# The split of the key, value and gate weights into high and low parts, made by GpSimd in place of VectorE

## The chip, the core and the metric

The kernel runs on one core of one Trainium2 chip. The metric is the time of one execution on the device in microseconds (us). Five engines work side by side on the core, each through its own list of instructions in order: TensorE (PE in the profile; its weight loads stand apart as PEld), VectorE (DVE), ScalarE (ACT), GpSimd (POOL) and SyncE (SP, which here only issues transfers). They wait for each other through semaphores.

## The reference

A gated mix of an attention with 32 heads that share one key and one value head, and a gated feed-forward network, over 2048 tokens of width 512:

```python
def _A_ref(x, wq, wk, wv, wo):                     # S = 2048, D = 512, H = 32, Dh = 16
    q = (x @ wq).reshape(B, S, H, Dh).transpose(0, 2, 1, 3)
    k = x @ wk
    v = x @ wv
    scores = jnp.einsum("bhqd,bkd->bhqk", q, k) * (Dh ** -0.5)
    p = softmax(scores, axis=-1)
    o = jnp.einsum("bhqk,bkd->bhqd", p, v)
    return o.transpose(0, 2, 1, 3).reshape(B, S, H * Dh) @ wo

def _B_ref(x, w_gate, w_up, w_down):               # F = 1792
    return (silu(x @ w_gate) * (x @ w_up)) @ w_down

g = sigmoid((x * gate_w).sum(-1, keepdims=True))
return g * _A_ref(x, ...) + (1 - g) * _B_ref(x, ...)
```

All inputs and the output are float32. The factors of the change are `wk` and `wv` (512 x 16 each) and `gate_w` (512).

## The kernel before

Each float32 factor of a product is split into a high part, rounded to the type float32r, and a low part, the difference between the factor and its high part. A product is then the sum of three matmuls: high by high, high by low, low by high. The helper `split(hi, lo, src, eng, eng_hi)` makes the parts with two instructions: a copy on `eng_hi` (L110, a CAST in the profile) and a subtraction on `eng` (L111, a TENSOR_TENSOR). Its defaults are VectorE for the copy and GpSimd for the subtraction.

The change lies in the kernel's opening, which is written out by hand from L675 on under a manual schedule: on each engine the instructions stand in the order of the code. The 2048 tokens are four chunks of 512. In this order:

- `zeros(WARM)` (L614) is 30 matmuls on zeros that fill TensorE's time until the first tokens have come.
- `load_wq(0)` loads the first 128 columns of the query weights into `wraw` and splits them on GpSimd into `wq0h` and `wq0l`, both steps.
- `transpose_x(c, i)` handles half a chunk, tiles `i` and `i + 1`: eight transposes on TensorE (L627) from `xt` into a PSUM tile `pss`, of which there are two; then ScalarE copies the tile to `xh` (L631) and VectorE subtracts to get `xl` (L632), which frees the PSUM tile. In chunk 0 six matmuls on zeros follow each four transposes.
- `prepare_kv()` stands between the two halves of chunk 0. It fills `wkv_h` and `wkv_l`, both 128 x 4 x 113, from `wkv_f`, which holds `wk`, `wv` and `gate_w` as they were loaded. There are four splits: the keys three times over as 128 x 4 x 48 into columns 0 to 47 and again into 64 to 111, the values (128 x 4 x 16) and the gate (128 x 4). That is four copies and four subtractions, all eight on VectorE.
- `project_kv(c)` multiplies a chunk by `wkv_h` and `wkv_l` (12 matmuls at L120): ScalarE copies the result to `vz` (L647), and GpSimd writes the keys' high and low parts into `ks` (L653, L655). `project_kv(0)` comes after both halves of chunk 1 have been transposed, and before chunk 2's transposes.

Then come the queries of the first eight heads (`query(0, c)`, L198, with `wq0h` and `wq0l`), and from about 50 us on the main part: scores (L760), exponentials (L771), the sums over the values (L787) and between them the feed-forward network's matmuls (L198).

A matmul that reads `wkv_h` waits until all four copies have been made, since its 113 columns hold what each of them writes; one that reads `wkv_l` waits for all four subtractions.

Of the kernel before, what the change touches and what calls it, by code (L numbers as in the profile page):

```python
# [65 lines left out]
def tile_gated_mix(ctx, tc, x, wq, wk, wv, wo, w_gate, w_up, w_down, gate_w, out):  # L66
    nc = tc.nc
# [41 lines left out]
    def split(hi, lo, src, eng=nc.gpsimd, eng_hi=nc.vector):  # L109
        eng_hi.tensor_copy(hi, src)  # L110
        eng.tensor_tensor(lo, src, hi.bitcast(F32), ALU.subtract)  # L111
# [459 lines left out]
    with tc.tile_pool(name="apool", bufs=1) as ap, tc.tile_pool(name="apool2", bufs=2) as a2:  # L571
# [9 lines left out]
        wkv_f = ap.tile([P, KD, 2 * DH + 1], F32, name="wkv_f")  # L581
# [6 lines left out]
        wkv_h = ap.tile([P, KD, KW], F32R, name="wkv_h")  # L588
        wkv_l = ap.tile([P, KD, KW], F32R, name="wkv_l")

        def prepare_kv():
            k, v, g = slice(0, DH), slice(DH, 2 * DH), slice(2 * DH, 2 * DH + 1)
            for r in (0, RT):
                to = [w[:, :, r:r + 3 * DH].rearrange("p k (i n) -> p k i n", i=3) for w in (wkv_h, wkv_l)]
                src = wkv_f[:, :, k].unsqueeze(2).to_broadcast([P, KD, 3, DH])
                split(to[0], to[1], src, nc.vector)
            for to, src in ((3 * DH, v), (KW - 1, g)):
                rows = slice(to, to + src.stop - src.start)
                split(wkv_h[:, :, rows], wkv_l[:, :, rows], wkv_f[:, :, src], nc.vector)

        spread = ap.tile([DH, DH, HG], F32, name="spread")

# [72 lines left out]
        with tc.manual_schedule():  # L675
# [5 lines left out]
            load_wq(0)  # L681
            transpose_x(0, 0)
            prepare_kv()
            transpose_x(0, 2)
            prepare_norms()
# [364 lines left out]
```

## Time and profile before

| | |
|---|---|
| median of 3 runs | 1328.92 us (1328.61 to 1329.1) |
| the profiled execution's own time | 1328.69 us |
| its span, first to last instruction | 1326.9 us |
| TensorE, matmuls | busy 1315.6 us, 99% of the span |
| VectorE | 805.4 us, 61% |
| ScalarE | 1077.5 us, 81% |
| GpSimd | 222.9 us, 17%, 229 instructions |

Times in rows of the trace count from the span's start. The timeline's rows give the start, the duration, the engine, the line, the operation and the tiles, and in brackets how long the engine was idle just before and what ended that. A matmul's end is modelled, and matmuls overlap, so that of a row of them the distance between starts tells the pace. The chain is the work that ended last, followed back from the last instruction; its rows in order of time give a start, a length, and the engine and line that filled it.

### The profile page before, as it was taken

The numbers are of one execution on the slowest core, as the hardware profiler recorded it, in microseconds if no ns is written. First come the engines' busy times: TensorE is split into PE (matmuls) and PEld (weight loads), VectorE is DVE, ScalarE is ACT, GpSimd is POOL, SyncE is SP. The second block draws the span as 40 slices with busy tenths as digits, with TensorE's granted clock in tenths as the row PEclk, the third lists the DMA queues.
The fourth block names the chain that finished last, engine by engine and source line by source line (L and its number), as shares of the span: only waits on it lengthen the run. The fifth ranks groups of instructions, "written<-read, shape, count | busy, mean of one in ns | idle before, by whom it ended". The sixth has DMA issues, their size and how long they took to land.

```text
span 1326.9 us, 26852 instructions
## 1 busy us (share of the span) xinstructions
PE 1315.6 (99%) x10767; PEld 786.2 (59%) x10767; DVE 805.4 (61%) x1370; ACT 1077.5 (81%) x1625; POOL 222.9 (17%) x229
## 2 busy tenths in 40 slices
PE   9999999999999999999999999999999999999998
PEld 7655565565555655555655555655555555655677
DVE  4655566566656666666656566566557566666642
ACT  4578888888888888888989889889889888889601
POOL 5350231142031151132110000000000000001043
PEclk9999999999999999999999999999999999999999
DMA  8677021221134373354134252143033252252264
GB/s 287 201 244 232 22 66 37 61 73 56 51 99 149 105 251 108 100 164 139 52 130 164 81 177 87 53 130 102 25 121 104 68 179 69 68 163 77 69 230 148
DMA packets 102513, 157.34 MB, mean 119 GB/s; under 512 B 11888, under 2 KB 43376, under 8 KB 100720
## 3 DMA queue, kind: packets, MB, share of 16 engines
q1 hardware_dynamic: 100656, 155.36, 36.0%
q8 instruction: 88, 1.44, 0.4%
q10 hardware_dynamic: 1728, 0.20, 0.1%
q14 instruction: 41, 0.34, 0.1%
HBM read 99.42 MB, written 55.57 MB: 117 GB/s over the span
## 4 chain that ended last, share of the span: by engine, by line
PE 97%; DVE 2%; ACT 1%; issue 0%; ACTq 0%; DVEq 0%
PE pf L198 38%; PE po L787 34%; PE pss L760 20%; PE pf L120 4%; ACT pt L771 1%; DVE pt L766 1%; PE pss L627 0%; PE po L614 0%; DVE acc L398 0%; DVE hh L110 0%; DVE xl L632 0%; DVE hl L111 0%; PE pss L667 0%; DVE ht L323 0%; DVE ht L333 0%
## 5 line engine op out<-in xcount | busy, mean ns | idle before, releaser
L771 ACT ACTIVATE pt<-pss 128x512 f32<-128x512 f32 (+1 forms) x1024 | 770.2, 814 | 159.9 <-PE pss L760 135.2
L766 DVE COPY pt<-pss 128x512 f32<-128x512 f32 x504 | 348.5, 692 | 366.9 <-PE pss L760 359.8
L787 PE MATMUL po<-pt,vaug 128*32 128x512 f32 x4096 | 461.4, 595 | 0.0
L760 PE MATMUL pss<-qs,ks 64*128 64x512 f32 x2048 | 411.4, 409 | 1.2 <-DVE sign L484 0.7
L760 PEld LDWEIGHTS pss<-qs,ks 64*128 64x128 f32 x2048 | 199.8, 184 | 184.0 <-ACT pt L771 116.5
L787 PEld LDWEIGHTS po<-pt,vaug 128*32 128x32 f32 x4096 | 124.7, 109 | 267.7 <-issue 266.2
L771 ACT ACTIVATE pt<-pt 128x512 f32<-128x512 f32 x504 | 282.0, 629 | 0.0
L198 PE MATMUL pf<-xh,wgh 64*128 64x512 f32 (+1 forms) x444 | 163.9, 393 | 0.5 <-DVE sign L484 0.3
L198 PE MATMUL pf<-xh,wgl 64*128 64x512 f32 (+1 forms) x444 | 164.2, 393 | 0.0
L198 PE MATMUL pf<-xl,wgh 64*128 64x512 f32 (+1 forms) x444 | 163.3, 391 | 0.0
L198 PE MATMUL pf<-xh,wuh 64*128 64x512 f32 (+1 forms) x440 | 160.3, 393 | 0.7 <-DVE sign L484 0.5
L198 PE MATMUL pf<-xh,wul 64*128 64x512 f32 (+1 forms) x440 | 160.2, 392 | 0.0
L198 PE MATMUL pf<-xl,wuh 64*128 64x512 f32 (+1 forms) x440 | 158.3, 391 | 0.0
L198 PE MATMUL pf<-wdh,hh 64*128 64x512 f32 (+1 forms) x411 | 136.4, 393 | 0.1
L198 PE MATMUL pf<-wdh,hl 64*128 64x512 f32 (+1 forms) x411 | 135.7, 391 | 0.0
L198 PE MATMUL pf<-wdl,hh 64*128 64x512 f32 (+1 forms) x411 | 135.4, 390 | 0.0
L798 DVE RECIPROCAL rsb<-rsb 128x128 f32<-128x128 f32 x128 | 116.6, 933 | 1.7 <-issue 0.7
L515 POOL CAST xh<-wraw 128x512 fp32r<-128x512 f32 x4 | 2.9, 732 | 497.0 <-PE pss L760 493.4
L198 PEld LDWEIGHTS pf<-xh,wgh 64*128 64x128 f32 (+1 forms) x444 | 78.9, 185 | 8.3 <-issue 1.1
L198 PEld LDWEIGHTS pf<-xh,wuh 64*128 64x128 f32 (+1 forms) x440 | 77.3, 185 | 10.8 <-DVE sign L484 1.4
L198 PEld LDWEIGHTS pf<-xh,wgl 64*128 64x128 f32 (+1 forms) x444 | 79.1, 185 | 5.5
L198 PEld LDWEIGHTS pf<-xl,wgh 64*128 64x128 f32 (+1 forms) x444 | 79.2, 185 | 5.4
(170 smaller groups left out, 1377.2 us busy)
## 6 DMA issues: line engine op xcount, KB each, us to landing
qs<-q_d SPq DMA_DIRECT2D x31, 512.0 KB, 4.6
q_d<-hh SPq DMA_DIRECT2D x28, 256.0 KB, 3.8
wraw<-in_B_w_gate_dram SPq DMA_DIRECT2D x28, 256.0 KB, 3.7
wraw<-in_B_w_up_dram SPq DMA_DIRECT2D x28, 256.0 KB, 3.2
wraw<-in_B_w_down_dram SPq DMA_DIRECT2D x28, 256.0 KB, 3.3
wgh<-w_d SPq DMA_DIRECT2D x28, 256.0 KB, 2.7
wgl<-w_d SPq DMA_DIRECT2D x28, 256.0 KB, 2.9
wuh<-w_d SPq DMA_DIRECT2D x28, 256.0 KB, 2.7
```

The source lines that it names most:

```text
L120: nc.tensor.matmul(ps, a, b, start=(i == 0), stop=(i == n - 1))
L198: ins = nc.tensor.matmul(self.ps, a, b, start=(i == 0 and opens), stop=(last and closes))
L515: nc.gpsimd.tensor_copy(OT[c][0][:, k, :], raw)
L760: nc.tensor.matmul(ps[:, b * CH:(b + 1) * CH], ks[rows, kt * P:(kt + 1) * P], QS[h][rows, j, :], start=True, stop=True)
L766: other = nc.vector.tensor_copy(pt[:, CH:], ps[:, CH:])
L771: ins = nc.scalar.activation(pt[:, w], ps[:, w], AF.Exp, scale=SCALE)
L787: ins = nc.tensor.matmul(po[c * 2 * DH:(c + 1) * 2 * DH, :], vaug[:, kt, :], pt[:, c * CH:(c + 1) * CH], start=(kt == 0), stop=(kt == NT - 1))
L798: nc.vector.reciprocal(rsb[:, w], rsb[:, w])
```

## The change

In `prepare_kv()` the two calls of `split` name GpSimd for both steps:

```diff
             for r in (0, RT):
                 to = [w[:, :, r:r + 3 * DH].rearrange("p k (i n) -> p k i n", i=3) for w in (wkv_h, wkv_l)]
                 src = wkv_f[:, :, k].unsqueeze(2).to_broadcast([P, KD, 3, DH])
-                split(to[0], to[1], src, nc.vector)
+                split(to[0], to[1], src, nc.gpsimd, nc.gpsimd)
             for to, src in ((3 * DH, v), (KW - 1, g)):
                 rows = slice(to, to + src.stop - src.start)
-                split(wkv_h[:, :, rows], wkv_l[:, :, rows], wkv_f[:, :, src], nc.vector)
+                split(wkv_h[:, :, rows], wkv_l[:, :, rows], wkv_f[:, :, src], nc.gpsimd, nc.gpsimd)
```

On VectorE the eight instructions are gone from between the first and the second `xl` of chunk 0. On GpSimd they come at the place that this piece of its list shows, in the opening (`wraw` is where loaded weights land, DMAHW names a wait for a transfer, Pool, DVE and Activation a wait for an instruction of GpSimd, VectorE or ScalarE):

```order
 L110 CAST wq0h<-wraw 128x512 [waits DMAHW1_49]
 L111 TENSOR_TENSOR wq0l<-wraw,wq0h 128x512 [waits Pool_49]
+L110 CAST wkv_h<-wkv_f 128x4x48 [waits DMAHW0_49]
+L111 TENSOR_TENSOR wkv_l<-wkv_f,wkv_h 128x4x48 [waits Pool_49]
+L110 CAST wkv_h<-wkv_f 128x4x48
+L111 TENSOR_TENSOR wkv_l<-wkv_f,wkv_h 128x4x48 [waits Pool_49]
+L110 CAST wkv_h<-wkv_f 128x4x16 [waits DMAHW2_49]
+L111 TENSOR_TENSOR wkv_l<-wkv_f,wkv_h 128x4x16 [waits Pool_49]
+L110 CAST wkv_h<-wkv_f 128x4 [waits DMAHW4_49]
+L111 TENSOR_TENSOR wkv_l<-wkv_f,wkv_h 128x4 [waits Pool_49]
 L653 CAST ks<-vz 48x512 [waits Activation_49]
 L655 TENSOR_TENSOR ks<-vz,ks 16x512 [waits Pool_49]
```

They stand behind the split of the first query weights, which waits for a transfer, and ahead of the first keys. TensorE's list keeps its order; its waits change where `project_kv(0)` begins:

```order
 L627 MATMUL pss<-ident,xt 128x128 [waits DMAHW0_49,DVE_49]
 L627 MATMUL pss<-ident,xt 128x128 x7
-L120 MATMUL pf<-xh,wkv_h 113x512 [waits Activation_49]
-L120 MATMUL pf<-xh,wkv_l 113x512
+L120 MATMUL pf<-xh,wkv_h 113x512 [waits Activation_49,Pool_49]
+L120 MATMUL pf<-xh,wkv_l 113x512 [waits Pool_49]
 L120 MATMUL pf<-xh,wkv_h 113x512
 L120 MATMUL pf<-xh,wkv_l 113x512
```

The first two matmuls on the key, value and gate weights now wait for GpSimd, where before the first one's wait for VectorE was already covered by the transposes ahead of it.

## The prediction

> **What bounds the kernel now.** I read the page first (busy shares, the chain by engine), then the waits of TensorE, then the chain in order of time through the opening, and last each engine's rows there.
>
> ```profile
> span 1326.9 us, 26852 instructions
> PE 1315.6 (99%) x10767; PEld 786.2 (59%) x10767; DVE 805.4 (61%) x1370; ACT 1077.5 (81%) x1625; POOL 222.9 (17%) x229
> PE 97%; DVE 2%; ACT 1%; issue 0%; ACTq 0%; DVEq 0%
> ```
>
> TensorE is the kernel: 97% of the chain. VectorE's 2% and ScalarE's 1% are places where TensorE stood still. Its waits over the whole span, all that the trace names:
>
> ```profile
> PE pss L627 <- DVE xl L632: 2.2, 2, 1.8
> PE po L614 <- DVE warm L678: 1.0, 1, 1.0
> PE pf L198 <- DVE sign L484: 0.8, 3, 0.3
> PE pss L760 <- DVE sign L484: 0.7, 3, 0.3
> PE pf L198 <- DVE hl L111: 0.4, 1, 0.4
> PE pss L760 <- ACT pt L771: 0.4, 2, 0.2
> PE pf L198 <- DVE hh L110: 0.3, 1, 0.3
> ```
>
> Only the first two lie in the opening (L627 are the transposes, L614 the matmuls on zeros). The other five sum to 2.6 us, and every releaser in them is an engine fed by TensorE itself. None is a transfer. So TensorE's list runs through almost without a break, and an idle microsecond put into it early is not given back later: all else in the kernel is released by TensorE's progress and moves along with it.
>
> The chain through the opening:
>
> ```profile
> 6.66 1.03 ACT xh L631
> 7.70 0.02 issue
> 7.72 1.23 DVE xl L632
> 8.95 0.18 DVE wkv_h L110
> ...
> 10.55 0.17 DVE wkv_l L111
> 10.72 1.14 DVE xl L632
> 11.86 0.04 issue
> 11.91 1.09 PE pss L627 x8
> 13.00 2.78 PE pf L120 x12
> 15.78 1.75 PE pss L627 x16
> ```
>
> The reader is to see two things. The eight instructions of the split are on the chain now: from 8.95 to 10.72 us, 1.77 us, they hold back the second `xl`, and that holds back the transposes of chunk 1's second half. And from 11.91 us on it is TensorE alone: transposes, `project_kv(0)` (12 matmuls), chunk 2's transposes.
>
> **What is taken away.**
>
> ```profile
> 8.34 1.02 ACT L631 ACTIVATE xh<-pss 128x1024 fp32r<-128x1024 f32 x1 [0.65 <-PE pss L627]
> 8.86 0.25 DVE L110 CAST wkv_h<-wkv_f 128x192 fp32r<-128x192 f32 x1
> 9.15 0.36 DVE L111 TENSOR_TENSOR wkv_l<-wkv_f,wkv_h 128x192 fp32r<-128x192 f32 x1
> 10.63 1.22 DVE L632 TENSOR_TENSOR xl<-pss,xh 128x1024 fp32r<-128x1024 f32 x1
> 11.91 1.09 PE L627 MATMUL pss<-ident,xt 128*128 128x128 f32 x8 [1.81 <-DVE xl L632]
> 13.07 0.39 PE L120 MATMUL pf<-xh,wkv_l 128*113 128x512 f32 x1
> ```
>
> Without the eight, the second `xl` waits only for its `xh`, which ends at 8.34 + 1.02 = 9.36. With the 0.03 us that the chain shows between the same two steps (6.66 + 1.03 to 7.72) it starts at 9.39 instead of 10.63, 1.24 us earlier, and ends at 10.61. The transposes of chunk 1's second half start some 0.06 us later (10.63 + 1.22 to 11.91), at 10.67, and are through at 11.76, if their tokens are there by then; the row names `xl` and no transfer as the last that they waited for, and a later landing would change nothing of the sum below. So TensorE could begin `project_kv(0)` 1.2 us earlier than now. What VectorE does next (`sel`, `spread`, `vaug`) only moves forward.
>
> **What is added.** GpSimd takes the eight after `wq0l`:
>
> ```profile
> 11.08 1.06 POOL L110 CAST wq0h<-wraw 128x512 fp32r<-128x512 f32 x1 [8.06 <-DMA wraw<-in_A_wq_dram]
> 12.22 1.56 POOL L111 TENSOR_TENSOR wq0l<-wraw,wq0h 128x512 fp32r<-128x512 f32 x1
> 16.48 0.61 POOL L653 CAST ks<-vz 48x512 fp32r<-48x512 f32 x1 [2.70 <-ACT vz L647]
> 17.16 1.28 POOL L655 TENSOR_TENSOR ks<-vz,ks 16x512 fp32r<-16x512 f32 x1
> ```
>
> The query weights land at 11.08, and nothing in the change touches that transfer. GpSimd is free at 12.22 + 1.56 = 13.78. That is the main point: even eight instructions of no length would be done 0.7 us after `project_kv(0)`'s second matmul starts today (13.07).
>
> Their length is not in the trace; no small copy or subtraction of GpSimd stands in it. The nearest rows:
>
> ```profile
> L111 POOL TENSOR_TENSOR wgl<-wraw,wgh 128x512 fp32r<-128x512 f32 x28 | 36.5, 1305 | 2.2
> L110 POOL CAST wuh<-wraw 128x512 fp32r<-128x512 f32 x28 | 17.2, 613 | 193.5 <-PE pf L198 141.2 <-DMA wraw<-in_B_w_up_dram 40.0 <-PE pss L760 12.3
> L608 POOL MEMSET ks<- 128x2048 f32 x1 | 1.8, 1811 | 0.0
> masks.py:197 POOL MEMSET ident<- 128x128 f32 x1 | 0.2, 206 | 0.3 <-POOLq L1036 0.3
> L1036 POOL MEMSET const-float32-0.0<- 128x1 f32 x1 | 0.1, 99 | 0.2 <-issue 0.2
> ```
>
> The memsets give a base of 0.1 us and (1811 - 206) / 1920 = 0.84 ns per element. A copy of 512 at 0.613 us is then 0.19 + 0.84 ns per element, and a subtraction with the same base 0.19 + (1305 - 190) / 512 = 2.18 ns per element. So 192 elements cost 0.35 and 0.61, 64 cost 0.24 and 0.33, 4 cost 0.19 and 0.20. The four splits sum to 2 x 0.96 + 0.57 + 0.39 = 2.88 us. The pattern in these eight is broken into runs of 16. `wq0h`, whose read jumps at every element, took 1.06 where a plain copy took 0.61; a little of that, and the 0.08 us from a copy's end to its subtraction (11.08 + 1.06 to 12.22), bring me to 3.0 us. The ends: cost in strict proportion to the elements, (192 + 192 + 64 + 4) / 512 x (0.61 + 1.30) = 1.7 us; or each of the eight as dear as a whole 512, 4 x 1.92 = 7.7 us. I stay by the sum because the small memsets are far below a 512's price.
>
> [...]
>
> **The sum.** The last subtraction ends at 13.78 + 3.0 = 16.8. The second matmul of `project_kv(0)`, the first on `wkv_l`, starts about 0.15 us later, at 16.95, in place of 13.07: +3.9 us. The first, on `wkv_h`, waits for the last copy, a step before, and decides nothing. After it TensorE's list runs as before: chunk 2's transposes, `vz`, the keys on GpSimd (idle there for 2.70 us before 16.48, and their release moves by the same 3.9), the query weights behind them. SyncE's list keeps its order; its loads of chunk 3 wait for chunk 1's transposes and go out earlier by 1.2 us, which nobody waits for. The 1.2 us won on VectorE is lost in TensorE's longer wait. Against the profiled execution, 1328.69 + 3.9 = 1332.6; its own time lies 0.23 below the median, so I forecast 1332.8 for the median, +0.29%.
>
> **The rivals.**
>
> *TensorE's clock falls in the new gap.* TensorE would stand still from 11.76 to about 16.6, 4.8 us. The longest gap in the trace so far is 1.81 us, and the pace behind it is full. At the start the pace was half:
>
> ```profile
> 1.00 3.38 PE L614 MATMUL po<-warm 128*128 128x128 bf16 x30 [1.00 <-DVE warm L678]
> 4.17 1.06 PE L627 MATMUL pss<-ident,xt 128*128 128x128 f32 x4
> 6.46 0.50 PE L614 MATMUL po<-warm 128*128 128x128 bf16 x6
> 6.80 0.61 PE L627 MATMUL pss<-ident,xt 128*128 128x128 f32 x4
> ```
>
> Four transposes took 1.06 us and later 0.61; the change falls near 6.4, 5.4 us after TensorE's first matmul. If the gap brings the slow pace back for as long, 5.4 us of work do half of it: 2.7 us more, 1335.5. For it: nothing in the trace shows a gap this long without it. Against: nothing shows that a gap does it. [...] I give this rival 0.32.
>
> *GpSimd's small instructions are cheap* (the other side: not slower by what can be told). The delay is the eight's length plus 0.9 us (13.78 + 0.15 - 13.07). At the strict proportion, 1.7 us, it is 2.6: 1331.5, +0.19%. It decides below 1.8 us for all eight, less than half the price that GpSimd's rows give when VectorE itself needed 1.77. Chance 0.11.
>
> *GpSimd does them in its idle 8 us.* The splits' data are loaded early, GpSimd idles until 11.08, and were they made then, `project_kv(0)` would start 1.2 us earlier: 1327.7. The engine's list decides: they stand behind `wq0h`, and the row shows that instruction waiting for its transfer. Chance 0.02.
>
> *They are dearer* than 4 us together, broken patterns costing a base per run: at the end of 7.7 us the delay is 8.6, 1337.5. `wq0h`'s 0.45 us extra for 64 broken rows speaks for less than 0.1 in 12 rows. Chance 0.05.
>
> **How the numbers follow.** The forecast itself has 0.49. What a measurement can tell from no change is about 0.2%, 2.7 us. Slower by more: 0.49 + 0.32 + 0.05 = 0.86; within: 0.11 + 0.02 = 0.13, since the idle time's 1.2 us are less than the bound; faster: 0.01, for what I have not thought of. The range goes from 1331.5, the proportional price, to 1336.0, the fallen clock's 1335.5 with half a microsecond for GpSimd's price; it leaves out the dear end and what lies below.
>
> **What the changed profile would show.** GpSimd's first `wkv_h` at about 13.7 and the last `wkv_l` ending at 16.8 (their sum 3.0); the second `xl` at 9.39; chunk 1's last transposes at 10.67; TensorE's new wait, about 4.8 us at L120 released by GpSimd's `wkv_l` or `wkv_h`; the second matmul at 16.95; from there every row later by 3.9, with no wait gone at the end. If the clock has fallen, the 12 matmuls behind the gap stand over 0.4 us apart in place of 0.23. The prediction is wrong if the query weights land at another time, if the eight take under 1.8 or over 4 us, or if a later stage takes up the shift.

## The result, and the profile after

| | before | after |
|---|---|---|
| median | 1328.63 us (1328.08 to 1329.1, 6 runs) | 1335.45 us (1334.37 to 1336.06, 6 runs) |
| ratio to before | | 1.0052, 95% interval 1.0042 to 1.0062 |
| the profiled execution's own time and span | 1328.69, 1326.9 us | 1334.83, 1332.8 us |
| mean granted clock of TensorE | 1.000 | 0.997 |

The change made the kernel 6.8 us slower. The forecast was 1332.8; the measured time is that of its first rival, the fallen clock, at 1335.5.

The page of the changed kernel, in the lines that answer to those of before:

```profile
span 1332.8 us, 26854 instructions
PE 1317.8 (99%) x10767; PEld 787.7 (59%) x10767; DVE 804.6 (60%) x1362; ACT 1077.1 (81%) x1625; POOL 225.0 (17%) x237
PEclk8999999999999999999999999999999999999999
```

The busy shares tell next to nothing: VectorE 0.8 us less, GpSimd 2.1 us more. The row of the clock, in tenths per fortieth of the span, does: its first digit is an 8. In the page of before it is a 9:

```profile
PEclk9999999999999999999999999999999999999999
```

The records of the clock begin with its rise (at 4.51 us here, at 6.39 in before), so the slow start of either execution is not in these rows or in the mean. TensorE's longest wait in the changed kernel is new:

```profile
PE pf L120 <- POOL wkv_h L110: 5.0, 1, 5.0
```

The chain in order of time shows what stands ahead of that wait and behind it:

```profile
4.70 6.03 DMA wraw<-in_A_wq_dram
...
10.79 1.06 POOL wq0h L110
...
11.93 1.51 POOL wq0l L111
13.44 0.30 POOL wkv_h L110
...
15.95 0.14 POOL wkv_h L110
16.09 0.04 issue
16.14 5.46 PE pf L120 x12
21.60 1.80 PE pss L627 x16
23.40 2.77 PE pf L120 x12
```

In the place of ScalarE, VectorE and TensorE the chain now has the transfer of the query weights, their split on GpSimd, and the eight instructions behind it. The 12 matmuls of `project_kv(0)` begin at 16.14 us and take 5.46 us; before they began at 13.00 and took 2.78, and the next 12 here take 2.77 again. The sum closes on the two profiled executions: 3.14 us later, 2.68 slower, 0.05 in the transposes, 5.87 of the spans' 5.9 us. The rest of the kernel adds nothing in sum: matmul for matmul the shift is 5.86 us at 33 us, up to 6.4 in between, and 5.84 at the last one.

Next comes the clock. The trace records the moments at which it changes: in the changed kernel at 4.51, 14.75, 21.58 and 1332.30 us. They lie 3, 2 and 384 times 3.413 us apart, and the two in before's trace, at 6.39 and 1327.35 us, 387 times. So the stretches below are steps of that grid (columns: stretch and length, busy time and count of TensorE's matmuls, of its weight loads, of VectorE, ScalarE and GpSimd, the granted clock, the transfers' share and GB/s):

```profile
11.34:14.75 3.41, 0.00 (x0) 0.00 (x0) 1.85 (x2) 0.82 (x1) 3.19 (x5) 1.00 0.96 332
14.75:18.17 3.42, 2.03 (x5) 1.63 (x6) 0.00 (x0) 0.00 (x0) 1.44 (x5) 0.50 0.32 117
18.17:21.58 3.41, 3.41 (x10) 2.37 (x9) 0.00 (x0) 0.00 (x0) 0.00 (x0) 0.50 0.00 0
21.58:25.00 3.42, 3.42 (x25) 3.02 (x24) 2.04 (x3) 2.87 (x4) 2.51 (x3) 1.00 0.00 0
```

TensorE did nothing from 11.34 to 14.75 us; then its clock stood at half for two such steps, and came back after one that was busy throughout. All six runs have a mean clock of 0.996 or 0.997; two steps at half speed in 1333 us make 0.997.

### The profile page after: what moved, and what is told of

The parts are those of the page before. It is cut to its first block, busy times and chain, and to the rows that moved or that the text cites. A ratio compares the mean times of both kernels' runs of the same rounds, so it can differ in the third digit from the quotient of the medians.

```text
span 1332.8 us, 26854 instructions
## 1 busy us (share of the span) xinstructions
PE 1317.8 (99%) x10767; PEld 787.7 (59%) x10767; DVE 804.6 (60%) x1362; ACT 1077.1 (81%) x1625; POOL 225.0 (17%) x237
## 4 chain that ended last, share of the span: by engine, by line
PE 96%; DVE 1%; ACT 1%; DMA 1%; POOL 0%; issue 0%; SPq 0%; ACTq 0%; DVEq 0%
PE pf L198 38%; PE po L787 34%; PE pss L760 20%; PE pf L120 4%; ACT pt L771 1%; DVE pt L766 1%; DMA wraw<-in_A_wq_dram 0%; PE pss L627 0%; DMA wkv_f<-in_A_wk_dram 0%; DVE acc L398 0%; DVE hh L110 0%; PE pss L667 0%; POOL wkv_l L111 0%; POOL wq0l L111 0%; DVE ht L323 0%
```

## The experiments

The theory from here on: the time is lost in two terms, 4.0 us because the split stands behind the query weights' transfer on GpSimd, and 2.7 us because TensorE's clock falls in the gap. The rival: the clock is a by-product, and GpSimd's pace or what follows it costs all of it.

### Zeros in the gap: fill60, fill20, fill40

```diff
             transpose_x(1, 2)
+            zeros(60)
```

> 60 matmuls on zeros are put into TensorE's wait of 5.0 us (11.10 to 16.14 us in the changed kernel's trace), ahead of the first matmul on the key, value and gate weights. At about 0.068 us each (six started 0.41 us before the next transpose) they take some 4.1 us, so that 0.9 us of the wait stay idle and GpSimd's end still decides. Theory (the gap halves TensorE's clock, and the 12 matmuls behind it take 5.46 us in place of 2.78): the 2.7 us come back, 1332.7 us, the 12 matmuls 0.23 us apart, mean clock 1.000. Rival (the slow matmuls are not due to the idle gap, or the time is lost elsewhere): 1335.4 us as before.

Measured: 1332.41 us (1331.15 to 1333.72, 7 runs), ratio 1.0029 (1.0018 to 1.0041) to the kernel before, whose median beside it was 1328.41: +4.0 us, where the change alone has +6.8; the two intervals, 2.4 to 5.4 us and 5.6 to 8.2, do not meet. TensorE's rows in its profile:

```profile
11.32 3.51 PE L614 MATMUL po<-warm 128*128 128x128 bf16 x60
16.36 0.48 PE L120 MATMUL pf<-xh,wkv_h 128*113 128x512 f32 x1 [1.53 <-POOL wkv_h L110]
...
16.97 0.39 PE L120 MATMUL pf<-xh,wkv_h 128*113 128x512 f32 x1
17.20 0.39 PE L120 MATMUL pf<-xh,wkv_l 128*113 128x512 f32 x1
```

The matmuls behind the gap start as late as in the changed kernel, and 0.23 us apart in place of 0.43; the granted clock is 1.00 in the two steps from 11.48 to 18.31 us. The two terms come apart: matmuls that compute nothing of use gave back 2.8 us, the 2.7 of the clock, and left 4.0 us. The rival falls.

> The same with 20 matmuls on zeros, some 1.4 us: a gap of about 3.7 us is left. If the clock falls only when a whole free-running window of 3.41 us (the distance that the records of the clock show) lies in the gap, it falls in about 1 execution of 10, and most runs stand at 1332.7 us with a mean clock of 1.000. If a mostly idle window is enough, as the fall in all six runs with a gap of 5.0 us suggests, it falls in part or all of the runs: those stand near 1335.4 us with a mean clock of 0.997. Rival of no link to the gap: 1335.4 us in all.

Measured: 1334.01 us (1333.35 to 1335.96, 5 runs), ratio 1.0042 (1.0028 to 1.0056). The profiled execution is the slowest of the five, at 1335.96 us. A gap of 3.67 us was left in it, and the clock fell for two steps, behind one that was busy for 20%:

```profile
12.43:15.84 3.41, 0.69 (x13) 0.52 (x10) 1.51 (x2) 0.64 (x1) 3.17 (x6) 1.00 0.96 312
```

So a mostly idle step was enough here, and it was not idle as a whole. The other four runs lie at 1333.35 to 1334.45 us, between the two cases. Whether the clock fell in each of them is not shown, since runs of fill60 reach 1333.72 us with a mean clock of 0.999 or 1.000.

> 40 matmuls on zeros in TensorE's wait, some 2.4 us by the 20 that took 1.28 us and the 60 that took 3.51: a gap of about 2.6 us is left. The profiles so far: the clock fell after a window of 3.41 us in which TensorE was busy for 38% or less (the windows' grid laid on its rows), and not after one with 45% or more. Theory (the fall goes by the share of a window): a gap of 2.6 us leaves a window at 24% at the lowest and 62% at the highest, by where the grid lies, so that the clock falls in part of the runs: these stand near 1335 us, the others at 1332.4 us, with the median between. Rival (a gap below a whole window never lets it fall): 1332.4 us in all.

Measured: 1333.58 us (1332.61 to 1334.24, 5 runs), ratio 1.0036 (1.0022 to 1.005). The gap left was 2.43 us, shorter than one step of 3.41, and in the profiled execution the clock fell all the same, for one step:

```profile
12.88:16.30 3.42, 1.17 (x21) 1.00 (x18) 1.22 (x1) 0.00 (x1) 3.18 (x8) 1.00 0.99 322
16.30:19.71 3.41, 3.23 (x8) 2.47 (x9) 0.00 (x0) 0.00 (x0) 0.34 (x2) 0.50 0.11 42
```

So the gap was not as long as a step either. Whether the clock held in others of its runs can't be read from their times, which lie between the two cases.

### Half of the change: sub_only

```diff
-                split(to[0], to[1], src, nc.gpsimd, nc.gpsimd)
+                split(to[0], to[1], src)
...
-                split(wkv_h[:, :, rows], wkv_l[:, :, rows], wkv_f[:, :, src], nc.gpsimd, nc.gpsimd)
+                split(wkv_h[:, :, rows], wkv_l[:, :, rows], wkv_f[:, :, src])
```

The copies are VectorE's again, and only the subtractions are GpSimd's.

> Half of the change: the four copies stay on VectorE, the four subtractions go to GpSimd. GpSimd is free of the query weights at about 13.4 to 13.8 us, and the four subtractions take 0.60 + 0.59 + 0.32 + 0.21 = 1.7 us: the second matmul on the new weights starts at about 15.3 us in place of 13.07. Theory: +2.2 us for the start, and a gap of about 3 us whose effect on the clock is open: 1330.8 us with the clock held, up to 1333.5 us with a fall. Rival (place in line does not matter, only the amount moved to GpSimd): half of the change's 6.8 us, 1332.0 us, at a full clock.

Measured: 1333.74 us (1332.23 to 1334.68, 4 runs), ratio 1.0039 (1.0024 to 1.0054). By the medians, half of the work costs about three quarters of the loss. The second matmul starts at 15.44 us behind a wait of 3.3 us, close to the 15.3 expected, and the clock fell with the dearer end of my figure. The step ahead of the fall is the busiest one in an opening that led to one, 1.33 us of 3.42, 39%:

```profile
10.37:13.79 3.42, 1.33 (x9) 1.00 (x9) 2.94 (x6) 1.91 (x2) 2.55 (x3) 1.00 0.91 298
13.79:17.20 3.41, 1.76 (x4) 1.37 (x5) 0.45 (x1) 0.00 (x0) 1.60 (x5) 0.50 0.79 299
```

Against it stand two steps of the kernel before on the same kind of grid, busy for 47% and 45%, behind which the clock held:

```profile
9.81:13.22 3.41, 1.60 (x13) 1.30 (x12) 3.34 (x10) 1.21 (x2) 2.05 (x2) 1.00 0.82 280
1320.53:1323.94 3.41, 1.54 (x13) 1.33 (x12) 0.97 (x2) 0.00 (x0) 0.00 (x0) 1.00 0.47 160
```

The end of a kernel, where no work is left to be slowed, narrows the bound. In kv_first, the next experiment, the clock fell at 1321.92 us, behind this step of 44%:

```profile
1318.51:1321.92 3.41, 1.50 (x13) 1.29 (x11) 0.97 (x2) 0.00 (x0) 0.00 (x0) 1.00 0.47 161
```

Of the steps at full clock that are measured here, the clock fell behind those busy for 0, 20, 34, 39 and 44%, and held behind those of 45% and 47% and behind one of 48% in another execution of before (before_look2, 7.31 to 10.72 us).

### GpSimd first the split, then the query weights: kv_first

```diff
-            load_wq(0)
             transpose_x(0, 0)
             prepare_kv()
+            load_wq(0)
```

> GpSimd makes the key, value and gate parts ahead of the first query weights (the load of the query weights is written behind the split; SyncE's list is the same). The last of their three loads lands at some 7.7 us, GpSimd then ends about 8.6 us, before chunk 1's transposes are through. Theory (the loss is GpSimd's place in line behind the wait for the query weights, not GpSimd's pace): no wait of TensorE on GpSimd, no fall of the clock, and the 1.2 to 1.9 us that VectorE's eight instructions held up are won: the first of the 12 matmuls at 11.1 to 11.8 us in place of 13.0, time 1326.7 to 1327.4 us. [...]

Measured: 1328.19 us (1326.57 to 1329.0, 11 runs), ratio 0.9998 (0.9989 to 1.0007). All of the loss is gone, with the same eight instructions on the same engine at the same length:

```profile
4.30 0.35 POOL L110 CAST wkv_h<-wkv_f 128x192 fp32r<-128x192 f32 x1 [1.28 <-DMA wkv_f<-in_A_wk_dram]
...
8.86 0.21 POOL L111 TENSOR_TENSOR wkv_l<-wkv_f,wkv_h 128x4 fp32r<-128x4 f32 x1
11.45 1.10 POOL L110 CAST wq0h<-wraw 128x512 fp32r<-128x512 f32 x1 [2.38 <-DMA wraw<-in_A_wq_dram]
```

They are done at 9.07 us, before TensorE wants them. The loss was the place in GpSimd's line. But the gain that I expected, 1.2 to 1.9 us, did not show.

> The same kernel as kv_first, which had a median of 1328.19 us over 11 runs and a profiled execution of 1326.82 us. Open is whether the 1.2 us that VectorE no longer holds up reach the end. Theory (they do, and the runs so far scatter by as much): 1327.2 us as a median of fresh runs. Rival (the transfers of the tokens set the transposes of chunk 1 in most executions, so that there was little to win): 1328.2 us, and the profile shows the transposes released by transfers.

Measured: 1328.39 us (1327.04 to 1329.99, 11 runs), ratio 0.9998 (0.9989 to 1.0007). The same again, nearer the rival's 1328.2 than the theory's 1327.2, and the profile has what the rival named (steps of issue, 0.02 to 0.04 us each, are left out):

```profile
2.13 5.60 DMA xt<-in_A_x_dram
7.77 0.67 PE pss L627 x4
8.46 1.03 ACT xh L631
9.52 1.24 DVE xl L632
10.80 1.09 PE pss L627 x8
11.89 2.78 PE pf L120 x12
```

Now the transfer of chunk 0's last tokens, landing at 7.73, begins the chain, and the 12 matmuls follow at 11.89 (11.97 in kv_first). That is 1.1 us ahead of the 13.00 of before's profile, which raises the question whether 13.00 is usual.

### Two more executions of the kernel before

> The kernel before itself, for a second profile of its opening. Open is why kv_first, whose 12 matmuls start at 11.7 us in both its profiles, is not 1.3 us faster than before, whose start at 13.0 us is known from one execution. If before's start comes earlier in other executions (where TensorE's clock rises early, the first transposes and with them VectorE's first subtraction come earlier, and the eight instructions behind it fit into the wait for the tokens), this one shows a start at 11.9 to 12.5 us. If 13.0 us is usual, the gain is lost behind the start.

> A third profile of the kernel before, with the same expectation as the second: a start of the 12 matmuls between 11.9 and 12.5 us where the clock rises before 5 us, and near 13.0 us where it rises after 6 us.

Measured: 1328.49 and 1327.36 us, one run each. Their chains, where the 12 matmuls begin:

```profile
11.05 1.09 PE pss L627 x8
12.14 2.78 PE pf L120 x12
```

```profile
10.84 1.09 PE pss L627 x8
11.94 2.77 PE pf L120 x12
```

The start is 12.14 and 11.94, as expected for an early rise of the clock: it rose at 4.6 and 3.9 us in them, against 6.4 in the execution on which the prediction was built, so that the first transposes and VectorE's first subtraction came earlier. What the eight hold up, by the end of the second `xh` and the start of the second `xl` behind it, is 0.1 us in the one, where the tokens came late (`xh` until 9.62, `xl` from 9.77), and 0.9 us in the other, where they came early (8.61 and 9.57), against 1.2 in the first. So there is less to win than one profile said, and kv_first, both of whose profiles have late tokens, wins 0.2 to 0.3 us in the medians, with an interval of 1.2 us to either side. How much of the rest reaches the end stays open.

### VectorE, but later in its line: dve_later

The kernel before with two lines exchanged:

```diff
-            prepare_kv()
             transpose_x(0, 2)
+            prepare_kv()
```

> The kernel before, with the split on VectorE but behind the second half of chunk 0, so that it no longer holds up that half's subtraction. The second subtraction then starts at about 9.4 us and the eight instructions run from about 10.6 to 12.4 us. The first matmul on wkv_h waits for the last copy, at some 12.2 us, in place of 13.0: theory (the place in VectorE's line was the cost, not the engine): 1327.6 to 1328.0 us. Rival (transfers set the pace): 1328.4 us, no difference.

Measured: 1332.07 us (1329.62 to 1333.28, 8 runs), ratio 1.0024 (1.0013 to 1.0034): slower by 3.4 us, against both expectations. VectorE's rows, and GpSimd's of the same stretch:

```profile
11.37 0.36 DVE L111 TENSOR_TENSOR wkv_l<-wkv_f,wkv_h 128x192 fp32r<-128x192 f32 x1
...
11.93 1.09 DVE L111 TENSOR_TENSOR wkv_l<-wkv_f,wkv_h 128x192 fp32r<-128x192 f32 x1
12.95 1.51 DVE L110 CAST wkv_h<-wkv_f 128x64 fp32r<-128x64 f32 x1
...
11.68 1.12 POOL L110 CAST wq0h<-wraw 128x512 fp32r<-128x512 f32 x1 [8.66 <-DMA wraw<-in_A_wq_dram]
12.89 1.51 POOL L111 TENSOR_TENSOR wq0l<-wraw,wq0h 128x512 fp32r<-128x512 f32 x1
```

The second subtraction of 192 took 1.09 us where the first took 0.36, and the copy of 64 took 1.51 where it took 0.19 before. Each started while an instruction of GpSimd ran, and ended just after it: 13.02 against 12.80, 14.46 against 14.40. The query weights' transfer had landed before both. The late start need not be all of the 3.4 us: five of the eight runs have a mean clock of 0.997 or 0.998, the profiled one 0.999, so the clock may have fallen in others, which no trace shows.

> In dve_later VectorE's subtraction of 192 took 1.09 us in place of 0.36 and its copy of 64 took 1.51 in place of 0.19; they ended 0.2 and 0.1 us after GpSimd's copy and subtraction on the first query weights, beside which they had started. Here the load of the query weights and with it GpSimd's two instructions are moved behind the first projection (SyncE issues that load behind the tokens' loads), so that GpSimd is idle beside VectorE's eight. [...] Rival (their length comes from the place in VectorE's line or from the transfers that land then): 1.09 and 1.51 us stay, 1332.1 us.

Against dve_later:

```diff
-            load_wq(0)
             transpose_x(0, 0)
...
             project_kv(0)
+            load_wq(0)
```

Measured: 1328.2 us (1327.79 to 1329.97, 10 runs), ratio 1.0001 (0.9992 to 1.0011): the rival's 1332.1 did not come. My own estimate was 1330.1, from dve_later's 1332.1 and its 2.0 us later start (14.94 against some 12.9), or down to 1328.5 if that profile's late end of the copies was in its other runs too.

```profile
11.83 0.36 DVE L111 TENSOR_TENSOR wkv_l<-wkv_f,wkv_h 128x192 fp32r<-128x192 f32 x1
12.11 0.19 DVE L110 CAST wkv_h<-wkv_f 128x64 fp32r<-128x64 f32 x1
12.78 0.45 PE L120 MATMUL pf<-xh,wkv_h 128*113 128x512 f32 x1 [0.56 <-DVE wkv_h L110]
```

With GpSimd idle beside them both have their usual lengths, and the matmuls start at 12.78 in place of 14.94. One of the two further executions of before has the same, where GpSimd's copy of the query weights came early; VectorE's small copy took 0.73 us in it, against 0.20 elsewhere, and ended at 11.73, just after GpSimd's at 11.66:

```profile
10.58 1.08 POOL L110 CAST wq0h<-wraw 128x512 fp32r<-128x512 f32 x1 [7.56 <-DMA wraw<-in_A_wq_dram]
11.00 0.73 DVE L605 COPY spread<-ident 16x128 f32<-16x128 f32 x1
```

So in these three rows an instruction of VectorE was held up until one of GpSimd that had started first was over: they ended 0.22, 0.06 and 0.07 us after it. What held them no trace shows.

No version beat the kernel before by more than the measurement can tell.

## Why the prediction was right or wrong

**The side: right. The size of the late start: right in its price, in part by luck in its sum.** GpSimd's eight instructions ran from 13.38 to 16.37 us, 2.99 us for the 3.0 forecast:

```profile
13.38 0.34 POOL L110 CAST wkv_h<-wkv_f 128x192 fp32r<-128x192 f32 x1
13.81 0.60 POOL L111 TENSOR_TENSOR wkv_l<-wkv_f,wkv_h 128x192 fp32r<-128x192 f32 x1
...
15.31 0.24 POOL L110 CAST wkv_h<-wkv_f 128x64 fp32r<-128x64 f32 x1
15.63 0.32 POOL L111 TENSOR_TENSOR wkv_l<-wkv_f,wkv_h 128x64 fp32r<-128x64 f32 x1
15.89 0.19 POOL L110 CAST wkv_h<-wkv_f 128x4 fp32r<-128x4 f32 x1
16.16 0.21 POOL L111 TENSOR_TENSOR wkv_l<-wkv_f,wkv_h 128x4 fp32r<-128x4 f32 x1
```

A base of 0.19 us with a price per element, from rows of other sizes, met the three sizes within 0.02 us; the rivals of cheaper and of dearer instructions fall with that. The +3.9 us of the forecast is the +4.0 that fill60 measured, where the clock held. But in the profiled execution the 12 matmuls began only 3.1 us later. The query weights' split began 0.3 us earlier than in before's profile, and the wait that ended last was the first matmul's for the last copy, which by the prediction "decides nothing", and not the second's for the last subtraction. What made up for it is that before's start at 13.00 was itself a late one, as told below under what VectorE would win; the prediction did not know that.

**No later stage gave it back: right.** The spans' difference is made up entirely by 22 us.

**The clock: the likeliest case was the wrong one.** The step that failed is the chance of 0.32: it was my estimate of how often such a gap brings the clock down, and no run shows what it was set by. What the runs showed in its place is a clock that fell behind steps in which TensorE was busy for 0% (the change), 20% (fill20), 34% (fill40), 39% (sub_only) and 44% (kv_first's end), and held behind 45% and 47% (before, busy time over 3.41 us in the rows above). An estimate from these steps: a gap of 5.0 us, split evenly over two of them, still leaves each 2.5 / 3.41 = 73% idle, so busy for 27% at the most, and by any other split one is less busy still. By that the fall was to be expected in every execution, and the six mean clocks, 0.996 and 0.997, agree; 1335.5 should have been the forecast.

The rival's price, 2.7 us, came true, but by luck. It was half of the 5.4 us that the start of before's trace ran at half pace (30 matmuls on zeros in 3.38 us, where fill60's 60 took 3.51), and that time differs from one execution to the next: from TensorE's first matmul at 1.00 us to the rise at 6.39 there, to 4.51 in the changed kernel, to 3.89 in before_look2. What set the price was the grid: the work began at 16.14 us, and the clock came back at 21.58, the end of the second slow step, 5.4 us later. First slow steps that were busy at half pace for 59% (the change), 52% (sub_only) and 72% (fill20) did not bring the clock back, and one of 95% (fill40) did.

**What VectorE would win: wrong in size, without effect.** The second `xl` did start earlier, at 8.63 us against 9.39 forecast and 10.63 before, and nothing came of it, as said. But the 1.24 us that I read off one execution went with a late rise of the clock; two others had 0.1 and 0.9, and kv_first, where the gain could have reached the end, showed none that its interval tells from zero. This puts the late start higher, too: the changed kernel's 16.14 is 3.1 us behind before's 13.00, but 4.0 and 4.2 behind the other two starts, and 4.0 or 4.2 with 2.7 is 6.7 or 6.9, about the 6.8 us that the medians show.

**The rival of GpSimd's idle 8 us** was ruled out by the list, rightly; kv_first is that rival built, and it takes the whole loss away. Its 1327.7 us was 0.5 to 0.7 too low, by the paragraph before this one.

## What to carry to other kernels

An engine with little to do is not free: what counts is what stands ahead of the moved work in its line, and here that was a transfer landing at 10.7 us, worth more than the slower engine; the same move with that load written behind it costs nothing that the measurement can tell. A wait put into TensorE's line was paid twice here, 4.0 us and 2.7, where it left one of these 3.41 us steps busy for 44% or less, so price a gap with the half-speed stretch behind it, and fill it with matmuls on zeros if it has to stay (in fill60 they gave back 2.8 us). Read the opening of a kernel in more than one execution before a microsecond of it enters a sum.

## What the runs showed of the hardware

- The clock's changes lay whole multiples of 3.413 us apart, on a grid that lay differently in the profiled executions (first rise between 3.89 us in before_look2 and 6.96 in sub_only): the lengths between changes were 3.41 us in fill40, 6.83 and 10.24 in the change, 1320.96, which is 387 steps, in before. In the steps measured it fell behind 0, 20, 34, 39 and 44% of matmul time and held behind 45, 47 and 48%, as far as the matmuls' modelled ends can tell. The kernel before stands close to the 44%, at 47% in its opening and 48% in that of before_look2.
- A gap of 2.43 us, shorter than a step, was enough for a fall in fill40's profiled execution.
- Once down, the clock stayed down for one step more behind steps busy for 52% (sub_only), 59% (the change) and 72% (fill20) at half pace, and rose behind those of 95% (fill40) and 100% (the change).
- GpSimd's small copies and subtractions of float32 cost, in the change, 0.19 to 0.21 us at 4 elements, 0.24 and 0.32 at 64, 0.34 and 0.60 at 192.
- A VectorE copy of 0.19 us took 1.51 us in dve_later, where a GpSimd subtraction of 1.51 us had started 0.06 us earlier.
